# A linear-attention and soft-MoE kernel on one core: the same tasks in another written order

## The chip, the cores and the metric

The program runs on one core of a Trainium2 chip, in one launch. The metric is device time in microseconds (us). The core has five engines with an instruction stream each: PE (TensorE, matrix multiplication), ACT (ScalarE), DVE (VectorE), POOL (GpSimd) and SP (SyncE, which here only issues transfers). Each engine takes its instructions strictly in the order in which the program gives them.

## The reference, cut to what matters

```python
# q, k, v: (batch 8, heads 8, seq 576, dim 64); w_phi: (64, 128)
def phi(x):
    proj = np.einsum('bhsd,df->bhsf', x, w_phi)
    proj = proj - np.max(np.abs(proj), axis=-1, keepdims=True)
    return np.concatenate([np.exp(proj), np.exp(-proj)], axis=-1)
q_p, k_p = (phi(q), phi(k))
kv = np.einsum('bhsf,bhsd->bhfd', k_p, v)
z = np.sum(k_p, axis=2)
num = np.einsum('bhsf,bhfd->bhsd', q_p, kv)
den = np.einsum('bhsf,bhf->bhs', q_p, z)[..., None] + 1e-06
x = num / den, tokens as rows: (4608, 512)
# soft MoE on x: 8 experts, 4 slots each, hidden size 1024
logits = x @ phi
d = softmax of logits over all tokens;  slot_input = d.T @ x
slot_out[e] = np.maximum(slot_input[e] @ w1[e], 0.0) @ w2[e]
c = softmax of logits over the 32 slots; return c @ slot_out
```

## The kernel before, in words

The 64 (batch, head) pairs are taken two batches at a time: 32 units of 1152 tokens, 9 tiles of 128 tokens each, so 288 tiles, in 72 blocks of 4 tiles. The work up to the first layer of the experts is written as some 1800 tasks. Each has a kind, a key and a function that issues its instructions. The kinds that matter here:

- `load` e (37 of them, SP): brings k and q of two blocks into the buffer `xs` (512 KB, line 173 through the helper `load`). There are three such buffers, so load e may start when `proj` 2(e-3)+1, the last reader of load e-3, has run. `proj` 2e and 2e+1 read load e.
- `vload` u (32, SP): the values of unit u into `vt` (325 KB). There are two buffers: vload u follows the last `vals` of unit u-2.
- `weight` i (30 of the 64 weight transfers wt, 512 KB, SP): expert weights into room that is free from the start. The other 34 come when a pool of buffers is closed (`close`): three when `xs` is done with (after `proj` 73), six when the k side is done with, and so on.
- `proj` b (74, PE, line 283): projection of k of block b (psk) and of q of block b-2 (psq), from 64 rows each. `kmax`, `kneg_exp`, `kpos_exp`, `kfac` (DVE, ACT) make the features of k and their factors, `vals` (POOL, line 303) multiplies values and factors into `vs`.
- `kvmm` p (96 pieces, three per unit, PE, line 330): k features times values, summed over the unit in one PSUM bank (kvp). `num` s (96, PE, line 383): q features times that sum (psn), three tiles each; `scale`, `comb`, `denom`, `recip`, `divide` (DVE, POOL) finish the attention.
- `turn`, `logits`, `dturn`, `slotsum` (PE) and their copies `xcopy` (ACT, DVE): the softmax over tokens and the slot sums, done for one of nine groups of 512 tokens whenever its rows are ready; the last three groups have names with f or z. `l1` is the first layer of the experts (line 873, hp), and what comes after it (lines 925 to 971: hidden rows, second layer yp, outputs pso, stores out) isn't planned but written out in the string `TAIL`.

The order of all planned tasks is one string, `ORDER`, with one letter for a task: the n-th occurrence of a letter is the n-th task of its kind. `Plan.run` goes through it and calls each function, so the string sets the order of each engine's instructions. It also sets which of the eight PSUM banks a task gets, since a task takes the bank that has been given back longest ago in the order of the string. The costs and due times in the `add` calls served a search outside of this file and have no effect here.

All SP transfers of this part go through one helper:

```python
def load(t, x):
    i = nc.sync.dma_start(t, x).ins
    if len(sent) > 5 and len(wpools) < 2:
        tc.add_manual_dep(i, sent[-2].name, ..., reason="deep")
    sent.append(i)
```

So, up to the first `close`, a transfer isn't issued before the second one ahead of it has landed: two are in flight at most. Behind a transfer that waits for this or for its buffer, all later ones wait too. From the first `close` on (weights 30 and up) this chain is off, and buffers alone hold a transfer back.

Of the kernel before, what the change touches and what calls it, by code (L numbers as in the profile page):

```python
# [57 lines left out]
class Plan:  # L58
# [42 lines left out]
ORDER = (  # L101
    "bcfdcfdbcbechkcghigifcllhnddaljkjiganmbojofqcjkhlddamuimlgfngpsmbjroqthvjrmfgbvjmkwrdgwnipvchfwyohckjmailnrokjdr"
    "zinmstmfjAlrvhvfpgiwdwvwjkobmqcgdAAacrbhnsgtyofmjllrivwknhqkvdzronjoxfviwxahAmicwfccgyzprdAjslhmgdktdAfihlAivjrm"
    "rnbakjmwnvloogvjxApmbwwqfsghcicAtfkrjdgrnmmlvyzvlhorwkqidfpwkcghnsvwjxacrnoxjAldyAmoiltjgqjArdfksnvrmzohwkivmmjA"
    "bxcgpwAcafhdmnivwAtlrdjvlmofwhggrpvkrniykfzqhjcvoawfhjnwbstiAycodczlgAAmdrjblgAknfirmdhoakrivAmnwvlgpovjkqjAwfwm"
    "mcnhiyzofABCBVVhAxcfbCljsArtmphvdrrwgkDvniwdaEBkiFVCjlcnvjHqoIBrC:gdmrsgwjmtjkromymvnfzVDhJGvliwpEKwbFoLcvwGHckf"
    "nIAyjd:AlcgKodlhfmqgflhzjbirbsLmaaiAtvrkwnvohpAAjrdcwkngifccqvjoldrhbiwAdsrmgklnymtvfhowjmzvljdwrkvgpjfnqimwkocn"
    "ocdsAAggMytrhfAhlrzviwmxjkabiArmnldcokvjfnqAwcvwdmpsglrlfjjdyothknaiqmAgavrmzhjivogwpJrkmjbxvNcjAfnAwoscdbhwlyrr"
    "tkAzdnmfovlvOxmakwhgrwpxngfvAowcdqyAzlijcghbjifsclMAtrhirknimokldvrnmvjwgqAmbovwAwAyzcApfhsiBtfCjBhjlAVcVkmndido"
    "CrlravgvrAfqwkmhjmfjkwvmgDwniBopdsEjgxVBynhCjFoCcHiIdcxafz:rbtmdglkGnvfowjVhmmrrvwNDvablwphEFyKLGkijcHgiAIq:cnbd"  # L110
    "lsJKrAjLlzofkhgimfAtnvorwmrvckwOxvwpcqndfhgcdjloyhmAidMijgrfdsmljgAArghkinaPtrjlfxkvnwmmhqkvvbwpjcildgoaznwcofmh"
    "jdsmrrAoiryxAafApkjhtlvzxAwijvmwJgvcjcwklqnbdofnmAmsdjyhxrAtvrzpofkAmrniwvPoglNvwqwkrcnsfjxhAacloAtxrigvxkddyjvb"
    "khmmrlznwiofAOcAvwhAgqnbfcpwojschtiralgddmkjfgnvgdwmjlyjrmlvipzhknfoxiwaxrmrorcgbhqvknAAfkAojstwmxvvyjwibnwzldrx"
    "mgAphBbBVCcoavCAlVDwfAijhkdBjEFiBVHCnxIGCccdqgV:molrslbyjMjDtkndKvEfzAmoLxhFqrrkwgvmmgAiHfvwPwIn:ocphfcJjjlyiKsr"
    "hlbtdgmmzdAavgMkGwLAnrfrqpvichkvajwioNwccAsnfAyomdhbdjtrzflgiAjAmrkllmvhgnobxrafkpwvnrjwdvAmkjiwqcyzdhgojcirmsft"
    "nlmkgnAovwvlpqdwrcofkhAjvwcdsjmnmgfoaiAylrtOzghrfknoivxjmApwrvwlvwjArqkPnhArcyiczsAtvRNRodvwkRlmSrghnAwjSSmAljvm"
    "4qkwpTRsRxQRySRUJnotrrSrzASSvwvTyROAMRvwUNzASowyyRzASAOzPASXTXQXYYXZWYZY0WZ2W0037629583523+568Q87+569855Q+8/+=iQ"
    "/=<!P!!Q!")

# [914 lines left out]
```

## Time and profile before

| | us |
|---|---|
| median of 3 runs (lowest, highest) | 328.63 (328.13, 330.14) |
| the profiled execution | 330.24 |
| its span, first to last instruction | 328.2 |
| PE busy in the span | 307.6 (94%) |
| DVE, ACT, POOL busy | 237.1, 228.6, 161.2 |

The profiled execution has 2.0 us around its span, and stands 1.6 us above the median of the runs. In the rows, PE is the matrix engine, PEld its loading of weights, SPq the SP queue of transfers, L173 line 173. An idle time stands in brackets with what released it; "issue" is idle time in which an engine waited for nothing that the profile shows.

### The profile page before, as it was taken

Reading aid. Unit: us, or ns where it says so; the run is one execution under the profiler, and the core shown is the slowest. Engines: PE = TensorE matmul, PEld = TensorE weight load, DVE = VectorE, ACT = ScalarE, POOL = GpSimd, SP = SyncE. Lnnn points to the kernel's source line nnn. Section 1 sums busy time; section 2 is a strip of 40 time slices with the busy share of each in tenths; the row PEclk is TensorE's granted clock in tenths of the full one; section 3 lists DMA queues with packets and bytes.
Section 4 is the critical chain, followed back from the end, with each engine's and each line's share of the span. In section 5 each row is a group of like instructions: output and inputs, shape, how many; then the busy total and the mean of one; then the engine's idle time right before and its main releaser. Section 6 shows DMA issues by size and latency. Waiting matters only on the chain.

```text
span 328.2 us, 16919 instructions
## 1 busy us (share of the span) xinstructions
PE 307.6 (94%) x7196; PEld 265.3 (81%) x7196; DVE 237.1 (72%) x688; ACT 228.6 (70%) x680; POOL 161.2 (49%) x339
## 2 busy tenths in 40 slices
PE   8899999899999999989999979899998999998970
PEld 4899999798889999987999879789998954385630
DVE  1777887758798989877978966878798767323460
ACT  3899899788698889868778957896796461013450
POOL 1466677673277686734577738267576400200000
PEclk9999999999999999999999999999999999999996
DMA  7475676653146166673757757765582998998896
GB/s 220 154 235 180 178 252 214 213 172 114 61 149 222 59 221 204 227 218 91 247 177 241 240 174 244 227 204 178 197 267 98 339 402 311 415 410 317 329 370 262
DMA packets 23419, 74.13 MB, mean 226 GB/s; under 512 B 2608, under 2 KB 2992, under 8 KB 23344
## 3 DMA queue, kind: packets, MB, share of 16 engines
q1 hardware_dynamic: 23120, 72.85, 64.8%
q8 instruction: 57, 0.93, 1.2%
q10 hardware_dynamic: 224, 0.20, 0.3%
q14 instruction: 18, 0.15, 0.1%
HBM read 63.60 MB, written 9.44 MB: 223 GB/s over the span
## 4 chain that ended last, share of the span: by engine, by line
PE 71%; DMA 15%; ACT 4%; DVE 2%; issue 2%; POOL 2%; SPq 1%; DVEq 0%; ACTq 0%; POOLq 0%
PE kvp L330 18%; PE psn L383 16%; PE psq L283 10%; DMA xs<-xT 9%; PE psk L283 7%; PE yp L947 5%; PE hp L873 4%; DMA vt<-vv 3%; PE pso L967 3%; DMA wt<-w 3%; PE psl L440 2%; PE pss L478 2%; PE psx L736 1%; POOL vs L303 1%; PE pss L587 1%
## 5 line engine op out<-in xcount | busy, mean ns | idle before, releaser
L303 POOL TENSOR_TENSOR vs<-vt,mk 128x520 f32<-128x520 f32 (+3 forms) x128 | 91.5, 732 | 50.8 <-ACT mk L292 28.5
L330 PE MATMUL kvp<-vs,kf 128*64 128x65 f32 (+1 forms) x2304 | 87.1, 229 | 0.0
L330 PEld LDWEIGHTS kvp<-vs,kf 128*64 128x64 f32 x2304 | 79.7, 138 | 4.1 <-POOL xn L429 0.8
L383 PE MATMUL psn<-kvs,qf 128*64 128x65 f32 x2304 | 80.5, 223 | 1.4 <-issue 1.3
L283 PE MATMUL psk<-wd,xs 64*128 64x128 f32 x576 | 74.4, 279 | 4.3 <-DMA xs<-xT 4.2
L383 PEld LDWEIGHTS psn<-kvs,qf 128*64 128x64 f32 x2304 | 73.7, 138 | 5.3 <-issue 2.8
L283 PE MATMUL psq<-xs,wd 64*128 64x128 f32 x576 | 73.8, 279 | 1.9 <-DMA xs<-xT 1.0
L283 PEld LDWEIGHTS psk<-wd,xs 64*128 64x128 f32 x576 | 66.9, 188 | 7.5 <-issue 5.0
L283 PEld LDWEIGHTS psq<-xs,wd 64*128 64x128 f32 x576 | 66.7, 188 | 4.1 <-issue 2.2
L288 DVE TENSOR_REDUCE mk<-psk 128x4 f32<-128x512 f32 x72 | 47.7, 673 | 16.0 <-ACT kf L314 11.9
L345 DVE TRANSPOSE_TENSOR_REDUCE mts<-psq 128x16 f32<-128x512 f32 x72 | 50.0, 704 | 7.3 <-PE psq L283 3.6
L314 ACT ACTIVATE kf<-psk 128x512 f32<-128x512 f32 x72 | 42.7, 594 | 16.6 <-PE psk L283 8.3
L350 ACT ACTIVATE qf<-psq 128x512 f32<-128x512 f32 x72 | 42.9, 597 | 10.7 <-PE psn L383 4.1
L429 POOL TENSOR_TENSOR xc<-un,dn 128x256 f32<-128x256 f32 x62 | 38.1, 616 | 12.8 <-DVE dn L414 7.8
L317 ACT ACTIVATE kf<-psk 128x512 f32<-128x512 f32 x72 | 43.0, 597 | 1.4 <-DVE mk L288 1.4
L353 ACT ACTIVATE qf<-psq 128x512 f32<-128x512 f32 x72 | 42.8, 596 | 0.1
L394 DVE TENSOR_TENSOR un<-psn,eq 128x195 f32<-128x195 f32 x96 | 33.2, 349 | 12.3 <-PE psn L383 8.9
L399 DVE TENSOR_TENSOR un<-psn,un 128x195 f32<-128x195 f32 x96 | 32.7, 351 | 1.2
L361 ACT ACTIVATE mh<-mts 32x36 f32<-32x36 f32 x128 | 29.3, 229 | 2.7 <-DVE mts L345 1.4
L367 DVE TENSOR_REDUCE eq<-mh 32x9 f32<-32x36 f32 x128 | 26.1, 204 | 4.5 <-ACT mh L361 3.2
L971 DVE COPY o<-pso 128x384 f32<-128x384 f32 x24 | 12.1, 551 | 13.6 <-PE pso L967 13.6
L291 ACT ACTIVATE mk<-mk 128x4 f32<-128x4 f32 x72 | 15.0, 208 | 8.3 <-DVE mk L288 7.3
(128 smaller groups left out, 301.7 us busy)
## 6 DMA issues: line engine op xcount, KB each, us to landing
wt<-w SPq DMA_DIRECT2D x64, 512.0 KB, 4.9
xs<-xT SPq DMA_DIRECT2D x34, 512.0 KB, 4.5
vt<-vv SPq DMA_DIRECT2D x32, 325.0 KB, 3.3
out<-o SPq DMA_DIRECT2D x24, 384.0 KB, 4.4
xs<-xT SPq DMA_DIRECT2D x4, 256.0 KB, 6.5
xs<-xT SPq DMA_DIRECT2D x1, 128.0 KB, 2.8
xs<-xT ACTq DMA_DIRECT2D x1, 128.0 KB, 3.1
cs<-cst SPq DMA_DIRECT2D x1, 128.0 KB, 2.7
```

What stands on the lines that cost most here:

```text
L283: nc.tensor.matmul(ps, l, r, start=True, stop=True)
L288: nc.vector.tensor_reduce(km[b][:, 2], kx[b], axis=AX, op=ALU.max, apply_absolute_value=True)
L303: nc.gpsimd.tensor_tensor(vs[b][:, :, place(b, u, t, o):place(b, u, t, o) + n], v[:, t + o:t + o + n].unsqueeze(1).broadcast_to([128, 2, n ...
L314: nc.scalar.activation(kf[b][:, 1], kx[b], AF.Exp, scale=-1.0)
L317: nc.scalar.activation(kf[b][:, 0], kx[b], AF.Exp)
L330: nc.tensor.matmul(ps[f:f + FE // 2, pn, o:o + m], kf[b][:, pn, NT * u + t - 4 * b, f:f + FE // 2], v2[:, pn, at:at + m], start=(t == 0 an ...
L345: nc.vector.tensor_reduce(mts.rearrange("p r j -> p j r")[:, o:o + 4], qx[b].rearrange("p j (r t) -> p (j r) t", t=32), axis=AX, op=ALU.ma ...
L350: nc.scalar.activation(qf[b][:, 0], qx[b], AF.Exp)
L353: nc.scalar.activation(qf[b][:, 1], qx[b], AF.Exp, scale=-1.0)
L383: nc.tensor.matmul(ps[64 * f:64 * f + 64, j, pn], q2[:, pn, 64 * f:64 * f + 64], kv[:, pn, b2], start=True, stop=True)
L394: nc.vector.tensor_tensor(un[u][:, CH * c:CH * c + CH], nx[s][:, :, 0], e[:, 1].unsqueeze(2).broadcast_to([128, CH, 65]), op=ALU.mult)
L429: divider(u).tensor_tensor(x[:, :, h * D:(h + 1) * D], un[u][:, a:b, 0:64], dn[u][:, a:b].unsqueeze(2).broadcast_to([128, b - a, 64]), op= ...
```

## The change

Only the string `ORDER` changes. All tasks are the same, 1801 letters before and after, each letter as often as before, and so are the functions, the chain in `load` and `TAIL`. The diff, cut:

```diff
 ORDER = (
-    "bcfdcfdbcbechkcghigifcllhnddaljkjiganmbojofqcjkhlddamuimlgfngpsmbjroqthvjrmfgbvjmkwrdgwnipvchfwyohckjmailnrokjdr"
...
-    "4qkwpTRsRxQRySRUJnotrrSrzASSvwvTyROAMRvwUNzASowyyRzASAOzPASXTXQXYYXZWYZY0WZ2W0037629583523+568Q87+569855Q+8/+=iQ"
-    "/=<!P!!Q!")
+    "bcecbbcdffhkdcanldgjkghficdagbkldhogiclmjgjidmfjmnpfhuqmblsjnriormtkhafjvrijwbvmhiaxovgwnocfchjwlqldpkgcdmmnjlfg"
...
+    "woAPrO4TokpRvqnUsRSwRRtrrySSSrzvAPwTUvyAwzAyzAXRvwYyzSAQRZA0SRQSX7XQX2TY3Y9Z6WWiYoZ0082523W763+5585<68+85Q859+/+"
+    "/==!!!QQ!")
```

Read by the letters' kinds, the order on SP from load 3 to load 12 is (L load, V vload, W weight, C constants):

```
before  L3 V2 C L4 L5 V3 L6 V4 L7 W0 W1 V5 L8 V6 W2 L9 W3 V7 W4 L10 W5 V8 V9 L11 L12
after   L3 C L4 V2 L5 V3 W0 W1 L6 L7 V4 V5 W2 L8 W3 W4 V6 L9 L10 V7 W5 L11 V8 L12
```

From load 19 to 21, from load 26 to load 30, and from load 33 to the first close:

```
before  L19 W8 L20 W9 V17 W10 L21
after   L19 W9 W10 V15 L20 V16 V17 L21
before  L26 V22 W15 V23 W16 L27 W17 W18 V24 W19 W20 L28 L29 V25 W21 V26 W22 L30
after   L26 V22 L27 V23 L28 W16 W17 W18 V24 L29 L30
before  L33 W26 L34 V28 V29 L35 L36 W27 V30 V31 W28 W29 close
after   L33 V28 W23 W24 W25 L34 V29 V30 W26 W27 L35 V31 W28 L36 W29 close
```

On PE 224 of the 336 places hold another task than before, mostly by a place or two. Around kvmm 18, around proj 22, between proj 51 and proj 56 (after alone), and at the end of the projections:

```
before  num14 proj16 proj17 num15 kvmm18 num16 num17 kvmm19 kvmm20 kvmm21 proj18
after   num14 kvmm18 proj16 proj17 num15 kvmm19 num16 num17 kvmm20 kvmm21 proj18
before  num20 proj20 proj21 proj22 kvmm24 num21 num22 kvmm25 num23 kvmm26
after   num20 num21 proj20 proj21 num22 kvmm24 num23 kvmm25 kvmm26 proj22
after   proj51 num60 num61 kvmm63 num62 kvmm64 kvmm65 proj52 proj53 kvmm66 kvmm67 num63 num64
        kvmm68 num65 num66 proj54 proj55 kvmm69 num67 kvmm70 kvmm71 proj56
before  kvmm80 kvmm81 dturn5 proj63 proj64 slotsum5 num78 (...) num89 num90 num91 proj72 proj73
after   dturn5 proj63 proj64 slotsum5 kvmm80 kvmm81 kvmm82 num78 (...) kvmm93 proj72 proj73 (...) num90 num91
```

## Rows read from the trace of the kernel before

**Rows 1.** Windows: start:end, length, busy PE, PEld, DVE, ACT, POOL, PEclk, DMA share, GB/s
```profile
4.90:62.00 57.10, 56.05 (x1406) 54.04 (x1407) 44.16 (x118) 49.82 (x150) 36.03 (x70) 1.00 0.65 207
62.00:192.00 130.00, 124.62 (x3191) 116.39 (x3191) 106.61 (x306) 106.06 (x321) 79.90 (x169) 1.00 0.56 178
192.00:251.00 59.00, 56.87 (x1455) 52.72 (x1455) 47.81 (x136) 46.78 (x143) 36.51 (x78) 1.00 0.63 202
273.00:317.00 44.00, 42.38 (x752) 24.07 (x755) 20.08 (x66) 10.92 (x27) 1.84 (x2) 1.00 0.94 361
```

**Rows 2.** Waits of PE over the span: us in total, times, longest us
```profile
PE psk L283 <- DMA xs<-xT: 4.2, 3, 2.5
PE psn L383 <- issue: 1.3, 2, 1.1
...
PE psq L283 <- ACT xT L763: 0.9, 1, 0.9
```

**Rows 3.** PE's timeline at four of these waits: start, us, what, [idle before <-releaser]
```profile
64.29 0.34 PE L283 MATMUL psk<-wd,xs 64*128 64x128 f32 x1 [1.41 <-DMA xs<-xT]
...
134.47 0.46 PE L283 MATMUL psk<-wd,xs 64*128 64x128 f32 x2 [0.27 <-DMA xs<-xT]
...
190.62 0.34 PE L283 MATMUL psk<-wd,xs 64*128 64x128 f32 x1 [2.50 <-DMA xs<-xT]
...
249.85 0.33 PE L383 MATMUL psn<-kvs,qf 128*64 128x65 f32 x3 [1.13 <-issue]
```

**Rows 4.** Chain that ended last, 172 to 191 us: start, us, what
```profile
172.49 4.67 DMA xs<-xT
...
185.50 5.00 DMA xs<-xT
```

**Rows 5.** What SP's queue waited for: us in total, times, longest us
```profile
SPq L173 <- DMA xs<-xT: 55.5, 27, 3.7
```

**Rows 6.** SP's timeline: load 7, and loads 11 and 12 in one row
```profile
28.59 0.33 SPq L173 DMA_DIRECT2D xs<-xT  x1
...
59.62 2.04 SPq L173 DMA_DIRECT2D xs<-xT  x2
```

**Rows 7.** Transfers of the page: count, KB each, median us from issue to landing
```profile
wt<-w SPq DMA_DIRECT2D x64, 512.0 KB, 4.9
xs<-xT SPq DMA_DIRECT2D x34, 512.0 KB, 4.5
vt<-vv SPq DMA_DIRECT2D x32, 325.0 KB, 3.3
```

**Rows 8.** Pieces of the chain that ended last: 24 matmuls of a num, 72 of kvmm
```profile
40.32 0.70 PE psn L383 x24
...
101.67 2.31 PE kvp L330 x72
```

**Rows 9.** Groups of the page: vals, and the psk half of proj
```profile
L303 POOL TENSOR_TENSOR vs<-vt,mk 128x520 f32<-128x520 f32 (+3 forms) x128 | 91.5, 732 | 50.8 <-ACT mk L292 28.5
...
L283 PE MATMUL psk<-wd,xs 64*128 64x128 f32 x576 | 74.4, 279 | 4.3 <-DMA xs<-xT 4.2
```

**Rows 10.** PE's timeline: kvmm 18; kvmm 19 to 21; kvmm 80 and 81; first of proj 72
```profile
50.47 0.64 PE L330 MATMUL kvp<-vs,kf 128*64 128x65 f32 x16
...
52.33 2.25 PE L330 MATMUL kvp<-vs,kf 128*64 128x65 f32 x64
...
217.70 1.10 PE L330 MATMUL kvp<-vs,kf 128*64 128x65 f32 x32
...
250.12 0.37 PE L283 MATMUL psq<-xs,wd 64*128 64x128 f32 x1
```

**Rows 11.** SP's timeline: loads 35 and 36, weights 28 to 63, first stores
```profile
227.47 2.14 SPq L173 DMA_DIRECT2D xs<-xT  x2
...
238.88 50.90 SPq L173 DMA_DIRECT2D wt<-w  x36
296.80 0.82 SPq L972 DMA_DIRECT2D out<-o  x2
```

More of the change, by code (lines that the diff above doesn't have):

```diff
@@ L101 @@
 ORDER = (
-    "bcfdcfdbcbechkcghigifcllhnddaljkjiganmbojofqcjkhlddamuimlgfngpsmbjroqthvjrmfgbvjmkwrdgwnipvchfwyohckjmailnrokjdr"
[L103 to L116, printed above, removed]
@@ L117 @@
-    "4qkwpTRsRxQRySRUJnotrrSrzASSvwvTyROAMRvwUNzASowyyRzASAOzPASXTXQXYYXZWYZY0WZ2W0037629583523+568Q87+569855Q+8/+=iQ"
-    "/=<!P!!Q!")
+    "bcecbbcdffhkdcanldgjkghficdagbkldhogiclmjgjidmfjmnpfhuqmblsjnriormtkhafjvrijwbvmhiaxovgwnocfchjwlqldpkgcdmmnjlfg"
+    "shtjyirmizxvkofpnhrrqvAwodwcjvwkcyrmbnAAdszgikmjtflvhownAdrvknbmroiflaogacApvwqgwhsdAyizcfcxbjjdhlrAikgtxmnjordl"
+    "klmnfjvqfhxwrgmhvvwpmcowiskgiacldAgrnyfArjtjmkojdmrvzlwAmjbbaqhivApswvnwkfhcnflohgcrkmAyftvlzidrojnqiAovwrgmkvxb"
+    "AjnjmdwhcwscmgjfalpoAhldrgtkqvnympdgorfhivjwrknzrivwwciyAcsrmjfddlgtohAkAzvirnjlmkwvfhvAiwAwmcAbcfyznokApoBdbBCa"
@@ new lines @@
+    "jhgVlrinmlqAgVrfsCjjkhtvmrmvoAwdvpDwEcnxaiFBxCGfwloBjHVCVdIcg:kycnhDliKqgdElaosjgtFmrkfnqhbjLvrmmprGvdbwwfkHzoic"
+    "hsvIjwl:dncKrbolimjgyAfqALakdnzJAmtrvwjgvwsgJhrfoAaimvjcpwAhkfcddlyxbAtcdnirljhvimkgmfMowzrjjlfAhgvnkmnwhrNqicgb"
+    "ovakwpjAclmydsflniAtjrzhgojvrqkommrwMvmbxipwdcAvwjyxAcsazAgfnhkfmdinllAtjrvhfkoqrwvAmjnoirwmogscdvltkpjNhwgicflm"
+    "yjAdfnrohrkvgidzkwbagvrvwnmwhAcniqaoAcdfcApjohryjzsmgldirtAbvgjkfhlnidgbmvxmkawwjfrjmhnopviojmwmlyAzOAAcpkbjBfla"
+    "qVhscCxBtdiCfVnrlvhoOrvwAkmrrvAwwknqgDdnjPEoBiVoCBcFCHGsVgcIl:tkdnfjDmvfowhyEirjzdmvmpFlwrhigvjxcHgkfJwIlcjKl:KG"
@@ new lines @@
+    "LAqstrdnhAgomdiAvfkLrhxbiyaMrjwmzAvvnpwAoqkxngcAwccdloslfjryghimdktljrdaznbogmkfnhvifqmphgrvwowvAcwkcsrrllinqAAo"
+    "jmkrytjdvbanjNzvskfAwowOAgjmndfhmclvboicgdmjpljAmwhrfdqayrtgkjifmvrnzpwhrhoiscAvwvkAwdtbxxcyjglngmxAjorzavfkbmmv"
+    "AnohjwclidAqkwfnAsoipchrdilgvftjrrdwbagkhrmyvzkAAJvMfjvwlwAnmmwnyzAooicBhikCAxadpBfnxCVVAjcPclhdigDqmosrEgFrlGfj"
+    "kgjntovvrmwdkjmBwhfpxlvwCjBVqnHicCIxr:ryazhbibsgrtvVdJmkmoDKfwnlvvoEAwAcjhgFHfwLbPIcja:xxijyclhKdkgqlGmdiMnmfmpr"
+    "jhfkgsomltiAhnorzvwjdprvqvwckcwnAoAcLlirsgfddxjAmyhgtfknbaijlromvzhdrkvifngghwlmwcvpdcjAoijkqmNwrrAnmfdOysPlgjma"
@@ L122 @@
+    "jhkoAptnJoilrxqknNfzjvxwmvrbwcMvwacAsxdglhAgykntofiAvrzrvdwAjAhbmwjvwmlxqfNmcAyogzOpchAiRslRSAjjktnRrSklrvSnmvmw"
+    "woAPrO4TokpRvqnUsRSwRRtrrySSSrzvAPwTUvyAwzAyzAXRvwYyzSAQRZA0SRQSX7XQX2TY3Y9Z6WWiYoZ0082523W763+5585<68+85Q859+/+"
+    "/==!!!QQ!")
 COLS = 128
```

## Prediction

> **What bounds the kernel now.** I read the windows first, one for each stage [rows 1]. From 4.9 to 251 us, where the attention runs, PE is busy for 56.05 of 57.10, 124.62 of 130.00 and 56.87 of 59.00 us: 8.6 us idle in 246, at a granted clock of 1.00, the level of 2.4 GHz. ACT and DVE stand at 80 to 87%, the DMA engines at 56 to 65%. So the matrix engine sets the pace, and what another order can win there lies in these 8.6 us, since the set of matmuls stays. The waits of PE come next [rows 2]: 4.2 us in three waits for a transfer into xs, 1.3 us in which it waited for nothing that is shown, 0.9 us for a copy into xT. PE's timeline puts them in place [rows 3]: 1.41 us before 64.29 (proj 22, which needs load 11), 0.27 before 134.47 (proj 42, load 21), 2.50 before 190.62 (proj 56, load 28), and 1.13 of "issue" before 249.85.
>
> Why are those loads late? In the chain that ended last, load 27 is issued at 172.49 and load 28 at 185.50, and each transfer between them leaves only as an earlier one lands [rows 4]. The buffer of load 28 had been free for long: load 25 is read for the last time by proj 51, more than fifteen us of PE work ahead of proj 56. SP's own waits say the same, 55.5 us for landings of xs alone [rows 5]. So this is a supply line with two transfers in flight. Its pitch can be read twice: load 7 leaves at 28.59 and load 11, fifteen issues later, at 59.62 [rows 6], 31.03 / 15 = 2.07 us an issue; loads 27 and 28 are six issues apart [rows 4], 13.01 / 6 = 2.17. That fits landings of 4.5 us for xs and 3.3 for vt with two in flight [rows 7]. A load is late when too many weights, which nobody needs before 270 us, stand ahead of it on SP.
>
> **The change, part by part.** *PE's work.* The tasks are the same, so the busy time stays. Entering and leaving proj costs a little, but the 74 projections fall into 38 runs instead of 39. I count nothing.
>
> *Load 11.* It now stands 12 issues behind load 7 instead of 15: 28.59 + 12 x 2.07 = 53.4, landed 4.5 us later at 57.9. Its reader proj 22 moves back behind num 22, num 23 and the nine tiles of kvmm 24 to 26, 2 x 0.70 + 2.31 = 3.7 us [rows 8]. Without its wait it would have begun at 64.29 - 1.41 = 62.9, so now at 66.6. A delay of 1.4 us becomes a margin of 8.7. Gain 1.4.
>
> *Load 28.* Weights 16 to 20 and vload 24 stand behind it instead of ahead. It can leave as soon as proj 51 is done. From proj 51 to proj 56 the new order has proj 51 to 55 at 74.4 / 72 = 1.03 [rows 9], eight num at 0.70 and 27 tiles of kvmm at 2.31 for nine [rows 8]: 5.2 + 5.6 + 6.9 = 17.7 us. Less the projection itself and 4.5 for the landing, 12 us of margin remain; even two further pitches on SP leave 8. Gain 2.5.
>
> *Load 21.* Weights 9 and 10 no longer stand between loads 20 and 21, two pitches or 4.1 us against a delay of 0.27. Gain 0.3. In sum the order takes away 4.2 us of waits.
>
> *What pays for it.* Three places lose their margin. (1) Weights 3 and 4 now go ahead of vload 6, which leaves seven issues after load 7: 28.59 + 14.5 = 43.1, landed at 46.4, and with a vals of 0.73 [rows 9] ready at 47.1. It is read by kvmm 18, which ran at 50.47 [rows 10] and moves ahead of two proj and a num, 2.8 us: 47.7. Margin 0.6 us. (2) vload 7, three issues on: 49.3, landed 52.6, ready 53.3; kvmm 21 ran 56 of 64 matmuls into the piece at 52.33, so at about 54.2. Margin 0.9. (3) Load 36 left within two us of 227.47 [rows 11] for a reader at 250.12 [rows 10], some 15 us ahead. Now weights 26 to 28 stand ahead of it, and it leaves twelve issues after vload 28. That one waits for vals of unit 26, done at the latest when kvmm 80 runs. The first of these issues follows at once (0.4), the rest at the pitch: 0.4 + 11 x 2.07 + 4.5 = 27.7 us after kvmm 80 at the latest. From kvmm 80 to proj 72 it was 250.12 - 217.70 = 32.4 us [rows 10]; take off 1.1 of issue, two proj and a slotsum of about 1 that now come before, and num 90 and 91 that now come after: 32.4 - 1.1 - 3.1 - 1.4 = 26.8. So 0.9 us late at worst, on time if vals runs a us or two ahead of kvmm. Each place costs PE nothing if the pitch holds, and one us for each us of slip. The ends are 0 and 3 us for the three together; I take 0.5, close to the lower end, since two margins are positive and the third is a worst case.
>
> One rule would lift this sum. The Trainium skill, page "DMA: Bandwidth & Descriptors", section "Anatomy of one DMA", fits a transfer as some 2.0 us plus its bytes at 436 GB/s (for the other issue path): an estimated 3.2 us for 512 KB. By that the pitch would be about 1.6 us, the three places would have margins of 4 us and more, and the sum 0.5 us better. The trace disagrees with medians of 4.5 and 4.9 us for these transfers [rows 7], so I keep 2.07.
>
> *The 1.13 us of issue.* It comes while weights crowd: weight 28 leaves at 238.88 and, with 30 and 31 off the chain, four are issued within four us [rows 11]. The new order keeps weights 29 to 31 close together behind load 36. It may recur (gain 0), go (1.1), or come twice (-1.1); I take half, 0.5.
>
> Here a page speaks against the gain. The Trainium skill, page "Runtime: NRT & Kernel Launch", section "Instruction fetch mechanics", says that a sequencer fetches its instructions in 16 KB blocks over its own DMA queue, mostly hidden. If the idle is such a fetch behind weights, the rule of hiding fails here by 1.13 us, and where it held, the wait would have another cause and stay: 0.5 us less gain.
>
> *Copies and banks.* The 0.9 us for xT [rows 2] arises at a proj right behind two turns, where a bank comes back only after a copy. That pattern (two turns of group 3, then proj 43) stands in the new order unchanged, and the bank hand-outs elsewhere are new. From -1.5 to 1; I take 0.
>
> *The tail.* Behind the last proj the buffers of xs open and 32 of the weights follow, then the stores; the DMA engines are 94% busy from 273 to 317 [rows 1]. These transfers start when proj 73 ends, and in the new order PE has some 0.6 us more to do between there and the first layer, so they aren't later against PE. Both ends of the tail move with the front, one for one.
>
> **Sum.** 4.2 - 0.5 + 0.5 = 4.2 us. Against the profiled execution that is 330.24 - 4.2 = 326.0; it stands 1.6 us above the median, so for the median 328.63 - 4.2 = 324.4. One per cent, about what a measurement tells here, is 3.3 us: 325.3 and 331.9 are the bounds.
>
> **Rivals.** *The idle moves on.* ACT is at 87% in the first stage [rows 1]; each wait of PE was also time in which ACT, DVE and POOL caught up, and with new bank hand-outs PE may wait for them instead. For it: nothing in the string protects these engines. Against: at 80 to 87% they have room on the mean, and PE waited for them little. Two thirds of the gain come back: about 327.2.
>
> *Slower.* The supply line slips at its new end. Landings of 4.1 us (twice the pitch) are assumed; at 5.4 each of the six rounds from vload 28 to load 36 takes 1.3 us longer, the load is 7.8 us late on a margin near zero, and proj 72, proj 73 and with them all weights of the tail wait: 328.63 - 4.2 + 7.8 = 332.2. The kernel is slower than before from landings of some 4.9 us on (six times 0.8 is more than 4.2). For it: weights land in 4.9 in the median [rows 7]. Against: that median holds the crowded tail, and the xs loads, two in flight, stand at 4.5.
>
> *All waits go,* the 1.3 of issue and the copies too: 4.2 + 1.3 + 0.9 + 0.4 = 6.8, so 321.8.
>
> **How the numbers follow.** The forecast, that the three waits go and little comes in their place, has 0.50; its own range is 322.9 to 326.0. The idle that moves on has 0.28, the slower case 0.10, the best one 0.12. Faster by over 1%: seven tenths of the forecast, the best case and a little of the second, 0.50. Slower by over 1%: most of the slower case, 0.08. Within 1%: 0.42. The range runs from 321.5, just under the best case, to 328.6, which takes in the second case up to no change and leaves out the slower one.
>
> **What would show it.** Right: no wait of PE for xs before proj 22, 42 and 56, SP issuing load 28 within a few us of load 27, PE's idle from 4.9 to 251 us down from 8.6 to 4 or 5, and the first matmul of the first layer four us earlier with the tail as long as before. Wrong: a new wait of PE for xs before proj 70 or 72, one at kvmm 18 or 21 behind POOL's vals, more waits for banks, or a longer tail.

## The result and the profile after

| | before | after |
|---|---|---|
| median of 16 runs (lowest, highest), us | 329.42 (328.13, 331.26) | 326.93 (324.22, 330.94) |
| the profiled execution, us | 330.24 | 328.58 |
| its span, us | 328.2 | 326.6 |
| ratio after to before, 95% interval | | 0.9906 [0.9878, 0.9934] |

The changed kernel is 0.9% faster: 2.5 us by the medians, 3.1 by the ratio. Ratios leave out disturbed executions, here and below, so they are not always the quotient of the medians beside them. The changed kernel also scatters more, over 6.7 us against 3.1.

The windows, in the columns of [rows 1], with the closing stretch from 251 to 273 us added; first the kernel after:

```profile
4.90:62.00 57.10, 57.03 (x1338) 54.98 (x1339) 41.59 (x110) 47.38 (x143) 34.30 (x68) 1.00 0.66 214
62.00:192.00 130.00, 128.46 (x3337) 120.86 (x3332) 111.09 (x317) 110.27 (x335) 83.41 (x173) 1.00 0.54 173
192.00:251.00 59.00, 57.24 (x1436) 52.93 (x1434) 49.28 (x141) 47.58 (x144) 38.27 (x81) 1.00 0.66 215
251.00:273.00 22.00, 19.28 (x344) 14.05 (x342) 13.40 (x53) 8.17 (x27) 2.46 (x7) 1.00 0.85 308
273.00:317.00 44.00, 43.04 (x758) 24.14 (x750) 20.98 (x69) 12.02 (x30) 1.84 (x2) 1.00 0.95 373
```

and the closing stretch of the kernel before:

```profile
251.00:273.00 22.00, 21.70 (x388) 16.28 (x384) 15.60 (x59) 11.24 (x34) 6.01 (x13) 1.00 0.87 326
```

From 4.9 to 251 us PE's idle fell from 8.6 us to 0.07 + 1.54 + 1.76 = 3.4. From 251 to 273 it rose from 0.3 to 2.7: half of the gain is handed back there. Busy PE is not always PE at work, though: the first window has 57.03 us busy with 1338 matmuls, where before it was 56.05 with 1406.

The waits of PE over the span, kernel after (columns of [rows 2]), say what went and what came:

```profile
PE psl L440 <- issue: 2.4, 2, 1.4
...
PE psq L283 <- DMA xs<-xT: 0.7, 1, 0.7
...
PE psn L383 <- ACT xT L763: 0.7, 2, 0.5
...
PE kvp L330 <- POOL vs L303: 0.2, 1, 0.2
```

The 4.2 us for loads 11, 21 and 28 are gone, with 0.7 left at another place. The 1.13 us of "issue" before 249.85 [rows 3] are gone too, and 2.4 us of the same sort stand at two other matmuls. PE's timeline puts them in place (columns of [rows 3]); the last row is the first layer:

```profile
245.75 1.68 PE L283 MATMUL psq<-xs,wd 64*128 64x128 f32 x16 [0.74 <-DMA xs<-xT]
...
254.65 0.85 PE L440 MATMUL psl<-xT,phs 128*32 128x128 f32 x20 [1.10 <-issue]
...
261.67 0.49 PE L440 MATMUL psl<-xT,phs 128*32 128x128 f32 x9 [1.35 <-issue]
...
272.69 2.78 PE L873 MATMUL hp<-wt,phs 128*32 128x512 f32 x24
```

and the first layer of the kernel before:

```profile
273.24 10.51 PE L873 MATMUL hp<-wt,phs 128*32 128x512 f32 x96
```

The three waits of the kernel after are on the path: the chain that ended last has them as pieces of their own (columns of [rows 4]).

```profile
240.77 4.85 DMA xs<-xT
...
253.56 1.10 issue
...
260.32 1.35 issue
```

The span in four stretches, from the starts of the same instructions in both timelines (us):

| stretch | before | after | change |
|---|---|---|---|
| start to kvmm 0 | 11.94 | 14.92 | +2.98 |
| kvmm 0 to proj 72 | 238.18 | 230.83 | -7.35 |
| proj 72 to the first layer | 23.13 | 26.94 | +3.81 |
| the first layer to the end | 54.98 | 53.87 | -1.11 |

Of the second and third line, 1.4 us are a mere shift: num 90 and 91 now stand behind proj 72 (two at 0.70 [rows 8]); eight matmuls of kvmm, under 0.3 us, went the other way. So the front gained some 5.9 and the closing stretch lost some 2.4, about the sum of its two issue waits (1.10 + 1.35).

The opening lost 3 us in another way. PE's timeline of the kernel after, twice from the first projections:

```profile
9.47 0.42 PE L283 MATMUL psk<-wd,xs 64*128 64x128 f32 x1
9.52 0.42 PE L283 MATMUL psq<-xs,wd 64*128 64x128 f32 x1
9.68 0.42 PE L283 MATMUL psk<-wd,xs 64*128 64x128 f32 x1
...
14.05 0.27 PE L283 MATMUL psk<-wd,xs 64*128 64x128 f32 x1
14.16 0.27 PE L283 MATMUL psq<-xs,wd 64*128 64x128 f32 x1
14.16 0.27 PE L283 MATMUL psk<-wd,xs 64*128 64x128 f32 x1
```

A psk every 0.21 us and 0.42 long, and later every 0.11 and 0.27 long: half the pace until about 13.4 us. The window over this stretch shows a granted clock of 1.00 (under e1 below), but the trace has no record of the clock before 13.39 us, and in e7 these matmuls have just this pace where the clock is on record at 0.50. The page's group for psk carries it, 77.5 us and 289 ns where [rows 9] has 74.4 and 279:

```profile
L283 PE MATMUL psk<-wd,xs 64*128 64x128 f32 x576 | 77.5, 289 | 0.0
```

### The profile page after: what moved, and what is told of

Its sections match the earlier page's. It is cut to its first block, busy times and chain, and to the rows that moved or that the text cites. A ratio compares the mean times of both kernels' runs of the same rounds, so it can differ in the third digit from the quotient of the medians.

```text
span 326.6 us, 16885 instructions
## 1 busy us (share of the span) xinstructions
PE 309.9 (95%) x7196; PEld 268.4 (82%) x7196; DVE 238.1 (73%) x688; ACT 228.1 (70%) x680; POOL 161.2 (49%) x339
## 4 chain that ended last, share of the span: by engine, by line
PE 87%; ACT 4%; DVE 3%; issue 2%; DMA 1%; POOL 0%; DVEq 0%; ACTq 0%; POOLq 0%
PE kvp L330 22%; PE psn L383 21%; PE psk L283 12%; PE psq L283 10%; PE yp L947 5%; PE hp L873 4%; PE pso L967 3%; PE psl L440 2%; PE psw L208 2%; DMA xs<-xT 1%; PE psx L736 1%; PE pss L478 1%; ACT kf L314 1%; PE pss L587 1%; PE psh L925 1%
## 5 line engine op out<-in xcount | busy, mean ns | idle before, releaser
L283 PE MATMUL psk<-wd,xs 64*128 64x128 f32 x576 | 77.5, 289 | 0.0
L283 PEld LDWEIGHTS psk<-wd,xs 64*128 64x128 f32 x576 | 70.2, 196 | 3.6 <-issue 1.5
L283 PEld LDWEIGHTS psq<-xs,wd 64*128 64x128 f32 x576 | 67.8, 192 | 2.5 <-PE kvp L330 0.9
L429 POOL TENSOR_TENSOR xc<-un,dn 128x256 f32<-128x256 f32 x62 | 38.1, 616 | 13.4 <-DVE dn L414 6.9
```

Source lines behind the costliest of these rows:

```text
L283: nc.tensor.matmul(ps, l, r, start=True, stop=True)
L429: divider(u).tensor_tensor(x[:, :, h * D:(h + 1) * D], un[u][:, a:b, 0:64], dn[u][:, a:b].unsqueeze(2).broadcast_to([128, b - a, 64]), op= ...
```

## The experiments

My theory after the result: the new order on SP brings the gain (no load is late), and the new order of the other engines gives part of it back between proj 72 and the first layer. Rivals: the gain comes from the other engines' order; the loss comes from the opening, whose first tasks are new; the loss comes from the crowd of weights behind proj 73, whatever the order.

Ratios are to the kernel before, run again beside each group of experiments. Its median was 329.4 us beside the result above and 330.7 to 331.2 beside the experiments, so the ratios compare better than the medians.

In the edits, "PE.." stands for the order of the tasks of PE, ACT, DVE and POOL, "SP" for that of the transfers.

**e1, the changed kernel once more.**

No edit.

> The changed kernel once more, nothing altered. In its first profile the matmuls of proj 2 to proj 4 came at half the pace of before (pairs 0.21 us apart, not 0.11) and the first kvmm began at 14.9 us instead of 11.9. Theory A (chance): the pace of the opening differs from execution to execution, so this profile may show either. Theory B (order): the new first letters cause it, so it comes again, with the first kvmm near 14.9. Both: about 0.99 of the time before, some 3 us less, and two waits of issue of 1.1 to 1.4 us between 250 and 265 us again.

Median 326.27 us, ratio 0.9869 [0.9815, 0.9923]; the profile's span is 322.6, 4.0 shorter than that of the same program above. kvmm 0 begins at 11.65 instead of 14.92. The windows of the two show the opening, first the kernel after, then e1 (columns of [rows 1]):

```profile
4.90:13.40 8.50, 8.50 (x61) 7.84 (x62) 2.42 (x4) 3.81 (x11) 0.80 (x1) 1.00 0.68 219
```

```profile
4.90:13.40 8.50, 8.27 (x134) 7.61 (x135) 5.00 (x8) 6.30 (x21) 2.85 (x5) 1.00 0.88 285
```

One program, 61 matmuls in 8.5 us in one execution and 134 in another: the half-paced opening is no property of the order alone. The issue waits, however, came again at the same two matmuls, with 2.8 us:

```profile
PE psl L440 <- issue: 2.8, 2, 2.0
```

**e2, the changed kernel with the first tasks of before.**

```diff
-    "bcecbbcdffhkdc...
+    "bcfdcfdbcbechk...
```

> The changed kernel with the first fourteen letters of before, so that the opening of PE is proj 0, 1, 2, spin, proj 3 as before. Theory B (order): the pace doubles early as before, the first kvmm is back near 12 us, and the kernel is about 3 us faster than the changed one, 0.982 of before. Theory A (chance): no difference to the changed kernel beyond 1 us in the median, and the profile may show a slow opening too.

Median 326.32, ratio 0.9846 [0.9797, 0.9895]: as e1. kvmm 0 began at 11.31, and proj 72 waited 1.9 us for load 36, with the granted clock at 0.50 for the 3.4 us behind it. The old first tasks bring no shorter median. Of the issue waits at `logits` this profile has only one of 0.5 us, with the same closing order as in e1.

**e3, the order of before, with only SP's from the changed kernel.**

```diff
 PE.. as before
-SP   L3 V2 C L4 L5 V3 L6 V4 L7 W0 W1 V5 L8 V6 W2 L9 ...
+SP   L3 C L4 V2 L5 V3 W0 W1 L6 L7 V4 V5 W2 L8 W3 W4 ...
```

> The kernel before with only SP's order of transfers taken from the change; PE, ACT, DVE and POOL keep their order. Theory (the transfers are what the change gains from): PE's waits for xs before proj 22, 42 and 56 go, 4.2 us in sum, and the time falls by 3 to 4.2 us, 0.987 to 0.991 of before. Rival (the waits only hid others, or the reordered engines do the gain): at least half of the 4.2 us comes back as other waits and the time is within 0.5% of before.

Median 323.74 (322.27 to 324.62), ratio 0.9787 [0.9748, 0.9827]: faster than the whole change, and by more than the 0.987 to 0.991 that I expected. The waits of PE:

```profile
PE psw L208 <- POOL call L204: 0.9, 1, 0.9
PE yp L947 <- issue: 0.9, 1, 0.9
PE psq L283 <- ACT xT L763: 0.9, 1, 0.9
...
PE kvp L330 <- POOL vs L303: 0.7, 2, 0.5
```

No wait for xs at all, none of issue ahead of the second layer. From kvmm 0 to the first layer it takes 256.02 us, and before 273.24 - 11.94 = 261.30: 5.3 less, which is the 4.2 of xs and the 1.1 of issue. With 0.4 us up to kvmm 0 and 1.1 from the first layer on the span is 6.8 shorter.

**e7, the mirror: the new order of the engines, SP's from before.**

```diff
 PE.. as in the changed kernel
-SP   L3 C L4 V2 L5 V3 W0 W1 L6 ...
+SP   L3 V2 C L4 L5 V3 L6 V4 L7 ...
```

> The change with SP's transfers put back into the order of before; PE, ACT, DVE and POOL as changed. Theory (the gain is the transfers'): waits for xs of 3 us or more come back, above all the one of some 2.5 us near proj 56, and the kernel is 3 to 5 us slower than the change, at or above the time of before (0.998 to 1.01). Rival (the other engines' order carries part of the gain): it stays at least 1.5 us below the time of before.

Median 339.58 (335.65 to 340.52), ratio 1.0334 [1.0257, 1.0411]. The wait of [rows 2] is back and doubled, and its longest piece, 5.27 us, stands at proj 56 as in [rows 3]:

```profile
PE psk L283 <- DMA xs<-xT: 8.7, 3, 5.3
...
194.97 0.55 PE L283 MATMUL psk<-wd,xs 64*128 64x128 f32 x1 [5.27 <-DMA xs<-xT]
...
195.53 0.42 PE L283 MATMUL psk<-wd,xs 64*128 64x128 f32 x1
...
195.75 0.42 PE L283 MATMUL psk<-wd,xs 64*128 64x128 f32 x1
```

I had expected a time near that of before; it is 3.3% above. The profile is 9.7 us longer than that of before: 3.1 of it is a half-paced opening, and the granted clock was 0.50 for 3.41 us twice, from 194.48 and from 211.55. The last two rows stand in the first of these stretches: 0.42 us for a psk and 0.22 from one to the next, the pace of the opening above (0.42 and 0.21). So the half-paced opening fits PE at the level of 1.2 GHz.

e3 and e7 together settle the first part: SP's order is the gain. With the old transfers the new order of the engines is slower than the old one.

**e5 and e6, the two halves of the engines' order.** Both with SP's order of the changed kernel. e5 has the new order of the engines up to proj 70 and the old one behind, e6 the old one up to proj 70 and the new one behind.

```diff
 SP   as in the changed kernel
 PE.. up to proj 70 as in the changed kernel
-     (...) kvmm93 proj72 proj73 (...) num90 num91
+     (...) num89 num90 num91 proj72 proj73
```

> SP's order of the change; PE, ACT, DVE and POOL in the changed order up to proj 70, and from there in the order of before. Theory (the changed order wins some 1 us more than SP alone on the way to proj 72, and loses it and 3 us more between there and the first layer): from proj 72 to the first matmul of the first layer it takes 22 to 23 us as in the run with SP's order alone, not 26 to 28, no wait of issue above 0.5 us falls there, and the kernel is as fast as that run or up to 2 us faster: 0.973 to 0.979 of before. Rival (the waits of issue come with an earlier front, whatever the order of the last groups): the waits of 2 us and more stay, and the time is that of the change, 0.987.

> The mirror of the run before: SP's order of the change, the other engines in the order of before up to proj 70 and in the changed order behind it. Theory (the changed order of the last groups draws the issue waits, since num 90 and 91 stand behind proj 73 and the weights crowd in as proj 73 ends): 25.5 us or more from proj 72 to the first layer, issue waits of 2 us or so, and 3 to 4 us slower than the run with SP's order alone, 0.987 to 0.991 of before. Rival: 22 to 23.5 us there and the same time as with SP's order alone, 0.979.

e5: median 323.12 (321.93 to 324.75), ratio 0.9843 [0.9791, 0.9895], in its profile 23.13 us from proj 72 to the first layer and no issue wait; it had the half-paced opening (kvmm 0 at 14.90). The ratio is above the 0.973 to 0.979 that I expected. e6: median 330.18, ratio 1.0033 [0.9983, 1.0084], with 0.6 us of issue at `logits` where I expected some 2. e6 isn't a clean mirror: where its halves meet, PE waited for values, once for

```profile
241.35 0.74 PE L330 MATMUL kvp<-vs,kf 128*64 128x65 f32 x16 [2.29 <-POOL vs L303]
```

and behind that wait the granted clock was 0.50, the level of 1.2 GHz, for 3.4 us. So e6 says little of the closing order by itself. e5 beats the changed kernel by 3.8 us in the median, but by 0.6 of a point in the ratio, some 2 us, at intervals that overlap.

**e4 and e8, the crowd of weights.** Behind the first close the chain is off. e4 lets four transfers be in flight there until the fourth pool closes, e8 two until the third.

```diff
-        if len(sent) > 5 and len(wpools) < 2:
-            tc.add_manual_dep(i, sent[-2].name, ...
+        if len(sent) > 5 and len(wpools) < 5:
+            tc.add_manual_dep(i, sent[-2 if len(wpools) < 2 else -4].name, ...
```

> The changed kernel, but the weights that follow the first close go out four in flight at most (each waits for the fourth one before it to land) until the fourth close, instead of up to ten. Theory (instructions of PE arrive late behind a crowd of weights): the two waits of issue between 250 and 265 us, 2.4 us in sum, fall below 0.8, the first layer starts some 2 us earlier, and the kernel is 1 to 2 us faster than the changed one. Rival (the issue waits belong to the new order of the last groups): they stay, and the time is the same or up to 2 us longer, since the weights land later.

> The change with the chain of two transfers in flight kept up to the third close, so that weights 30 to 38 go out two at a time instead of up to seven. Theory (PE's instructions are late behind the crowd of weights): the issue waits between 245 and 265 us, 2.4 and 2.8 us in the two profiles of the change and 1.6 with four in flight, fall below 0.6, and the first layer begins 2 us earlier after proj 72; the gain at the end is 0 to 2 us, as the weights land later. Rival (the waits belong to the order and not to the transfers): 2 us and more of issue remain.

e4: 325.55, ratio 0.9869 [0.9815, 0.9924]; issue waits 1.6 us behind proj 72, not under 0.8 as expected. e8: 324.98 (12 runs), ratio 0.9884 [0.9844, 0.9923]; no issue wait behind proj 72. Its first waits:

```profile
PE psq L283 <- DVE cd L508: 1.1, 1, 1.1
PE psw L208 <- POOL call L204: 0.9, 1, 0.9
```

In e8 the closing stretch takes 24.32 us instead of 26.94, but from the first layer to the end it is 55.56 instead of 53.87: PE meets no wait for a weight there, but from its last matmul to the end, while the stores go out, 10.0 us pass instead of 8.7. So 1.7 of the 2.6 us are given back, and as a remedy the thinner crowd is worth little. As a test it is weak: one profile, in which proj 72 had waited 1.1 us for `cd`, so that PE came later to the two matmuls by itself (more on this below), and e2, with the crowd, had 0.5 us of these waits.

**e9 and e10, the first tasks exchanged in e5 and e3.** e9 is e5 with the first eleven tasks of the engines of before, e10 is e3 with those of the changed kernel.

```diff
 e9
-PE.. c e c c d f f h k d c ...
+PE.. c f d c f d c e c h k ...
 e10
-PE.. c f d c f d c e c h k ...
+PE.. c e c c d f f h k d c ...
```

> The order of e5 (the new order up to proj 70, the old one behind, SP as in the changed kernel) with the first eleven PE, ACT, DVE and POOL tasks in the order of the kernel before. Theory (the half-paced opening of the changed kernel's profile comes by chance, whatever the first tasks are): the median is that of e5, 323.1, within 1 us; a profile with the full-paced opening has kvmm 0 at 11.9 and its span some 3 us under the 322.9 of e5. Rival (the new first tasks raise the chance of a slow opening, which in e5's median stands for one to two us): the median falls to 321 to 322, and the runs scatter less.

> The order of e3 (engines as before, SP as in the changed kernel) with the first eleven PE, ACT, DVE and POOL tasks in the order of the changed kernel. Theory (chance): the median is that of e3, 323.7, within 1 us, and kvmm 0 begins at 11.6 to 12. Rival (the new first tasks bring the slow opening): kvmm 0 at 14.9 or so in the profile, and a median 1 to 3 us above e3's, 325 to 327.

e9: median 324.20 (322.39 to 329.09), ratio 0.9800 [0.9739, 0.9861]. e10: 324.87 (324.14 to 328.64), ratio 0.9875 [0.9811, 0.9940]. kvmm 0 began at 11.41 and 11.66, both at full pace. The rival of e9 (a median of 321 to 322) isn't borne out. e10 is less clear: its profile shows full pace, but it stands 1.1 us above e3 by the median and 0.9 of a point, some 3 us, by the ratio, which is what its rival gave. Four of its six runs took 324.1 to 324.9 us and two 328.4 and 328.6; a slow opening in the two would explain that, but no profile of them shows it. What I had not expected is in the profile of e9, whose closing order is that of before:

```profile
252.34 0.85 PE L440 MATMUL psl<-xT,phs 128*32 128x128 f32 x20 [2.39 <-issue]
259.73 0.60 PE L440 MATMUL psl<-xT,phs 128*32 128x128 f32 x10 [1.64 <-issue]
```

4.0 us, at the same two matmuls of `logits`, and 27.92 us from proj 72 to the first layer. So the old closing order doesn't exclude these waits.

**e11 and e12, the programs of e9 and e5 once more.**

No edit.

> The program of e9 once more. Theory (the two issue waits at flogits, 4.0 us in e9 and none in the nearly equal e5, are a matter of the single execution, as is the half-paced opening): a profile that shows another sum of them, 0 to 2 us, with proj 72 to the first layer shorter than 27.9 us by just that, down to 23.1 us without them. Rival (the order with the full-paced opening meets them always): 3 to 4 us of them again at the same two places, and 27 to 28 us.

> The program of e5 once more. Theory (single execution): either of the two may differ from e5, which had the half-paced opening (kvmm 0 at 14.9) and no issue wait; a profile with kvmm 0 at 11.5 or with issue waits would show it. Rival (this program always opens at half pace and never waits there): kvmm 0 at 14.9 and 23.1 us from proj 72 to the first layer again. Both give a median of 323 within 1 us, equal to that of the program of e9 run beside it within 1 us.

e12: median 322.16 (320.89 to 328.12), ratio 0.9752 [0.9713, 0.9792], the fastest kernel of the study. Its profile has the full-paced opening (kvmm 0 at 11.45) where e5, the same program, had the slow one, and no issue wait behind proj 72; the two matmuls that waited elsewhere run here as one block each:

```profile
250.63 0.86 PE L440 MATMUL psl<-xT,phs 128*32 128x128 f32 x24
...
255.53 1.07 PE L440 MATMUL psl<-xT,phs 128*32 128x128 f32 x30
...
267.49 7.93 PE L873 MATMUL hp<-wt,phs 128*32 128x512 f32 x72
```

e11: median 323.64 (321.38 to 330.80), ratio 0.9791 [0.9737, 0.9844]. Its profile has the waits again:

```profile
253.67 0.85 PE L440 MATMUL psl<-xT,phs 128*32 128x128 f32 x20 [2.85 <-issue]
...
261.61 0.60 PE L440 MATMUL psl<-xT,phs 128*32 128x128 f32 x10 [2.20 <-issue]
```

Against my expectation (0 to 2 us) that is the rival's number, and 30.49 us to the first layer. Behind the second wait the window shows the granted clock (columns of [rows 1]):

```profile
262.70:266.10 3.40, 3.40 (x31) 3.01 (x32) 1.12 (x5) 1.90 (x4) 0.64 (x1) 0.50 0.60 231
```

The closing stretch of e11 is 7.4 us longer than those without a wait, of which 5.0 are the waits; most of the other 2.3 falls to the clock. The profiled executions of e9 and e11 took 327.30 and 330.80 us and others of their programs 322.39 and 321.38, so I take no comparison of orders from these two profiles. The medians of the two programs, 1.1 and 1.5 us apart at overlapping intervals, decide nothing.

**What the twelve together show.** Starts from PE's timelines, in us; issue is the wait at `logits` behind proj 72; "c" marks kernels in which num 90 and 91 (1.4 us) stand behind proj 72:

| | to kvmm 0 | to proj 72 | to first layer | to the end | issue |
|---|---|---|---|---|---|
| before | 11.94 | 238.18 | 23.13 | 54.98 | 0 |
| after, c | 14.92 | 230.83 | 26.94 | 53.87 | 2.4 |
| e1, c | 11.65 | 230.25 | 27.64 | 53.05 | 2.8 |
| e8, c | 11.98 | 232.01 | 24.32 | 55.56 | 0 |
| e3 | 11.57 | 232.89 | 23.13 | 53.82 | 0 |
| e10 | 11.66 | 233.58 | 23.09 | 53.19 | 0 |
| e5 | 14.90 | 231.67 | 23.13 | 53.17 | 0 |
| e12 | 11.45 | 232.92 | 23.12 | 53.92 | 0 |
| e2, c | 11.31 | 233.23 | 26.62 | 53.78 | 0.5 |
| e4, c | 12.03 | 230.55 | 26.46 | 54.50 | 1.6 |
| e6, c | 11.90 | 237.95 | 26.13 | 53.80 | 0.6 |
| e7, c | 15.01 | 243.03 | 25.63 | 54.24 | 0.8 |
| e9 | 11.41 | 231.88 | 27.92 | 54.20 | 4.0 |
| e11 | 11.77 | 232.41 | 30.49 | 54.24 | 5.0 |

Where there is no issue wait the closing stretch is 23.1 us (22.9 in e8, less the 1.4); where there is one, it is longer by about the wait and up to 0.8 more, in e6 by another wait of 0.9 (behind `num`), and in e2 and e11 by the clock, 1.6 and 2.3 us. So the new closing order costs little by its work, and my theory's second half falls in the form I gave it. Whether the order sets how often the waits are met can't be read from these profiles: with it PE waited 0 to 2.8 us in seven of them, with the old one on SP's new order not at all in four and 4.0 and 5.0 us in two, the long executions of e9 and e11. By the ratios it may cost something: 0.985 to 0.991 with it (e2, e4, e1, after), 0.975 to 0.984 without it on the same front (e12, e11, e9, e5), on the mean some 0.8 of a point or 2.5 us. But one program gave 0.975 and 0.984 (e12, e5), so this is likely and not shown. And from kvmm 0 to proj 72 the new order of the engines has no clear gain over the old one: 231.7 to 232.9 (e5, e9, e11, e12) against 232.9 and 233.6 (e3, e10). What is sure of the 5.9 us in the front came with SP's order; a us or so of it, at most, is the engines'.

## Why the prediction was right, and where it wasn't

The forecast was 324.4 us in a range of 321.5 to 328.6; 326.93 lies in it, a gain of 2.5 to 3.1 us instead of 4.2, and just short of the one per cent that I gave 0.50.

*What bounds the kernel, and the three loads: right, and shown.* PE's idle fell from 8.6 to 3.4 us by the end of the front, where I had said 4 or 5. Proj 22, 42 and 56 started without a wait. SP's timeline of the kernel after shows the step for load 28, the third row here, behind load 27 and vload 23:

```profile
166.56 0.40 SPq L173 DMA_DIRECT2D xs<-xT  x1
173.37 0.33 SPq L173 DMA_DIRECT2D vt<-vv  x1
173.79 0.38 SPq L173 DMA_DIRECT2D xs<-xT  x1
```

It left 7.2 us behind load 27 instead of 13.0, landed at 177.87 by the trace's landings, and proj 56 began at 187.40: 9.5 us of margin, where I worked out 8 to 12. Load 11 landed at 58.66 for a proj 22 at 70.19. That the order on SP does this, and does it without the engines' new order, is what e3 and e7 show.

*The three tight places: right.* Load 36 was to land at most 27.7 us behind kvmm 80, and proj 72 to need it 26.8 behind: 0.9 us late. kvmm 80 began at 217.98 and the load landed at 245.61, 27.6 behind; proj 72 waited 0.74. The parts were off and cancelled: vload 28 left 2.4 us ahead of kvmm 80, and the pitch up to load 36 was (240.77 - 215.95) / 11 = 2.26 us instead of 2.07. With 0.19 more for each of eleven issues, a place worked out to half a us was luck. At kvmm 18 and 21 no wait appeared; all waits for vs sum to 0.2. I took 0.5 for the three, and they cost 0.7; in the other profiles with the new order of the engines up to proj 72, load 36 cost 0 (e1, e4, e8) to 1.9 (e2).

*The issue: the step that failed.* "It may recur (gain 0), go (1.1), or come twice (-1.1); I take half, 0.5." It came twice and more: gone at its old place, 2.4 and 2.8 us behind proj 72 in the two profiles of this program. The term was a loss of 1.3 to 1.7 us instead of a gain of 0.5, some 2 us off, more than the whole gap between forecast and result. I had put it down to the crowd of weights and bounded it by the one wait that I saw; the price was set by a row of another place and another moment. The forecast of the rest was if anything too low: e3 and e10, which have SP's order and no issue wait at `logits`, gain 2.1 and 1.2%, some 7 and 4 us.

Here the page that I weighed needs its answer. The Trainium skill, page "Runtime: NRT & Kernel Launch", section "Instruction fetch mechanics", has a sequencer fetch its next 16 KB of instructions over its own DMA queue and calls that mostly hidden. The trace agrees on the blocks: the 57 packets of the instruction queue have 16,384 bytes each.

```profile
q8 instruction: 57, 0.93, 1.2%
```

It also says what the waits are. In the fourteen profiles PE has 43 issue waits of 0.15 to 2.85 us, and every one ends 1.2 to 1.7 us after the end of one of these packets, which come some 5.7 us apart on the mean (326.6 / 57). In the profile of after the packets end at 253.09 and 260.29 and PE goes on at 254.65 and 261.67. In e3, e5, e10 and e12, without a wait, the packet had ended 2.4 to 4.1 us ahead of the same two matmuls; in e8 it had ended 1.47 and 1.46 ahead, so that e8 met no wait by a hair. By this timing PE waited for its instructions, and what the page calls mostly hidden isn't hidden at these places.

What makes a packet late stays open. Weights in flight are one candidate: of the kernels with the new closing order e8, with two, has the second packet soonest behind the matmul that needed the first, 3.8 us against 4.8 to 5.6 in the other six. But they don't decide alone: SP issues them at nearly the same times in e12 (239.87, 240.25, 240.72, 246.11) and in e11 (240.38, 240.76, 241.22, 245.89), and e12 has no wait where e11 has 5.0 us. Waits of up to 0.56 us stand in the front too, where two transfers are in flight at most (e12, ahead of 179.39). No run held a fetch back by itself, and e5, e9, e11 and e12 differ in nothing but the first eleven tasks.

*PE's work, copies and banks, tail: as costed, within a us.* The front ends 5.9 us sooner against the 4.2 of xs less 0.7, the 1.1 of issue and some 1.3 more; that rest lies in places that I set to nothing, with -1.5 to 1 as bounds, and e5 and e12 (1.25 us apart with one program) say that it is no larger than the scatter. Waits that I read as copies and banks did rise, from 1.5 us (0.9 for xT, 0.6 for eT) to 2.1 in six waits: the sign "more waits for banks" came, at 0.6 us. Behind proj 73 PE had 48 matmuls of num more and 8 of kvmm fewer, some 1.2 us and not 0.6. The tail from the first layer on is 1.1 us shorter, in e3 too (1.2), where the engines' order is the old one; of the 1.1, 0.7 is an issue wait in the second layer (0.9 before, 0.2 after).

*The opening: not foreseen.* 3 us of the profiled execution, the largest single miss in it: 5.9 and 1.1 gained, 2.4 and 3.0 lost make the 1.6 us by which this profile is shorter than that of before. By e1 and e12 it is no fixed part of the change: the profiles with the new first tasks have it in 3 of 8 (after, e5, e7), those with the old ones in 0 of 6. Whether the new tasks raise the chance can't be read from so few; the medians of e2 and e9 show no gain from the old ones, and e10 against e3 leans the other way. Without the slow opening the profile of after would have ended at about 323.6, near e1's 322.6. How much of the gap of 1.1 to 1.7 us between forecast and medians is the opening and how much the issue isn't known, since the other runs have no profile.

*The rivals.* "The idle moves on" is nearest to the result in time (327.2) but not in its mechanism: it isn't ACT, POOL or banks that PE waits for, but "issue". "Slower" has its place right, as load 36 is the tightest point, but its landing took 4.85 us and not 5.4; e7 shows a supply line that slipped, with 8.7 us of waits. "All waits go" at 321.8 is near what e12 comes to (322.16), but that is another order of tasks, beside a kernel before of 330.7, and so no more than a coincidence. One reading of mine was off without effect: DVE stood at 77% in the first stage (44.16 of 57.10 [rows 1]), not at 80 or more.

## What to carry to other kernels

When a planner's order is searched anew, separate the queue of transfers from the engines' order and measure each alone: here the transfers' order alone was worth 2.1 and 1.2% (e3, e10), and the whole search 0.9 to 1.5% (after, e1, e2). A load is late because of what stands ahead of it on its queue, so count the issues between it and the event that frees its buffer, times the measured pitch, and where the margin is a small part of that sum, the pitch may decide (here it was 9% longer than reckoned, 2.1 us over eleven issues). An idle time that is released by nothing in the profile is worth a look at the packets of the instruction queue; here it was to be priced from zero to several times the row seen, not at half of it.

## What the runs showed of the hardware

- PE can run its first 8 us at half pace: 0.42 us a matmul instead of 0.27, 61 matmuls where another execution of the same program has 134. It is the pace that e7 shows where the granted clock is on record at 0.50, the level of 1.2 GHz. The column of the granted clock shows 1.00 for the opening, but the trace's first record of the clock, at 1.00, is at 13.39 us in that execution, where full pace begins, and at 13.36 and 13.57 in e5 and e7, which opened like it; in the others it lies between 3.6 and 6.7.
- Around some waits of PE the granted clock fell to 0.50 (1.2 GHz) for 3.41 us: in e2 behind 1.92 us, in e6 behind 2.29, in e7 at the end of 5.27 and behind 3.02, in e11 behind 2.20, but not behind the 2.85 of e11, the 2.50 of before, the 2.39 of e9 or the 2.02 of e1. In the closing stretches of e2 and e11 this cost some 1.6 and 2.3 us on top of the waits.
- PE can wait for its own instructions, and the profile calls it "issue": 43 such waits in fourteen profiles, up to 2.85 us long, each ending 1.2 to 1.7 us after a 16 KB packet of the instruction queue. At the same two matmuls of `logits` they came to 2.4 and 2.8 us in after and e1 and 4.0 and 5.0 in e9 and e11, and came not at all in e5 and e12, which differ from e9 and e11 in the first eleven tasks alone.
